# Cluster similarities of q and k in full float32, in four strips of 32 array columns

## The chip, the cores and the metric

The kernel runs on one core of a Trainium2 chip. Its engines are TensorE (PE in the rows, PEld for its weight loads), VectorE (DVE), ScalarE (ACT), GpSimd (POOL) and SyncE (SP), which here only issues DMAs. The metric is the device time of one execution in microseconds (us), as the median of several runs. The profile is of one execution of its own.

## What is computed

Clustered attention (2 batches, 8 heads, 768 positions, head size 64), followed by two gated feed-forward stages. The change touches the first lines of the attention only.

```python
q_n = q / (np.linalg.norm(q, axis=-1, keepdims=True) + 1e-06)
k_n = ...                                    # as q_n
c_n = ...                                    # the 16 centroids of each head
q_assign = np.argmax(np.einsum('bhsd,hcd->bhsc', q_n, c_n), axis=-1)
k_assign = np.argmax(np.einsum('bhsd,hcd->bhsc', k_n, c_n), axis=-1)
mask = q_assign[:, :, :, None] == k_assign[:, :, None, :]
scores = np.where(mask, scale * np.matmul(q, k.transpose(0, 1, 3, 2)), -1e9)
attn = softmax(scores)
x = attn @ v
...                                          # (x @ w1) * (x @ w2) @ w3 @ w_out, then the gated stage
```

A position belongs to the cluster whose centroid has the largest similarity. Positive factors of q and k don't change an argmax, so the kernel normalizes the centroids alone.

## The kernel before

**Pairs and blocks.** The 16 heads of both batches are handled as 8 pairs of heads (`pr` 0 to 7, the two heads `e` 0 and 1 on partitions 0 to 63 and 64 to 127). A block is 256 queries of one head; a pair has six, `at` 0 to 5, and the loop of L561 runs over 48 blocks `i` and a few more that fill and empty the pipeline. Each pass of the loop writes the instructions of all engines in a fixed order by hand, and each engine runs its own in that order.

**One block.** TensorE makes the scores of 128 queries at a time: `scores(2i+3)` at the start of the pass, `scores(2i+4)` in its second half, four matmuls each into one PSUM tile `s` (L323 to L326). DVE takes the row maximum `nm` (L333), ACT the exponential `e` (L344). TensorE transposes `e` (L354, tiles `pt`, three groups of four), ACT and DVE or GpSimd split the transposed weights into a high part `ph` (rounded to the short format fp32r) and a low part `pl` (L372, L383, L54, L59), and TensorE multiplies both by the values (L395, L396, tile `av`). ACT copies `av` out (L404). Products of fp32r parts stand in for float32 products all through the kernel.

**PSUM buffers.** The scores and the similarities take turns in one pool, `ps_s`, of two buffers. A tile waits until the last reader of the tile before last is done: normally the exponential of the scores two tiles earlier.

**Preparing a pair.** q and k of a pair are loaded as `raw` (L175; L172 for pair 1), and split into high and low parts `hi`, `lo` (`prep_split`, L191; for pair 1 into unused room of `x_hl`, `prep_split_1`, L206). SP moves the parts into the operand tiles `QH`, `KH`, `QX`, `KX` of each head (`prep_scatter`, L217). The similarities (`prep_sims`, L240) are eight matmuls from the parts and the centroid weights `cw`. `cw` has, for q and for k, 32 columns a head: 16 of the centroids' high part and 16 of their low part. The result `sims` has 128 rows (q and k, two heads, two parts) of 768 positions. DVE transposes it in squares of 32 (L255), the two parts are added (L261, on DVE for pair 0, else on GpSimd), and an argmax with its one-hot code follows (L268 to L282). The one-hot `oh` is padded to 32 columns a head and position group and transposed back (L286, `ohT`). `prep_mask` (L289) brings 32 rows of it under q's rows in `QH` and 32 under k's rows in `KH`, as 0 and a large negative number, so that the scores of other clusters fall far below. Pair 0, head 0 does this on ACT and DVE, everything else by DMA after one GpSimd operation (L300).

**When.** For pair `later`, two ahead of the running one, the load is issued at `at` 0, the split is made at `at` 3 and 4, the similarities at the end of `at` 5. For the next pair, DVE's transpose follows at `at` 0, the argmax at 1, the one-hot at 2, the masks at 3. Pair 0 is prepared before the loop, pair 1 in its first passes: its similarities stand in pass -1.

**Weights of the later stages.** They arrive as 64-bit words and are converted in the background of the attention (`f64_steps`, L88 to L120). For the first matrix DVE uses the unused end of a score tile in PSUM as scratch (L106 to L108), in the passes `at` 4 and 5 of pair 0.

Of the kernel before, what the change touches and what calls it, by code (L numbers as in the profile page):

```python
# [27 lines left out]
def tile_cluster_attention__then__moe__then__gated_moe(  # L28
# [123 lines left out]
    chi, clo = early[:, 256:384].bitcast(F32R), early[:, 384:512].bitcast(F32R)  # L152
    for j in range(2):
        nc.sync.dma_start(c2[:, j, :], centroids.rearrange("h c d -> (h c) d"))
    cw = cent.tile([128, NP, 2, 128], F32R, name="cw")
    nc.gpsimd.memset(cw.bitcast(F32), 0.0)
    dec = cent.tile([128, C], F32, name="dec")
    nc.gpsimd.iota(dec, [[-1, C]], base=C, channel_multiplier=0, allow_small_or_imprecise_dtypes=True)
    oh = cent.tile([128, S // 32, 32], F32, name="oh")
    nc.gpsimd.memset(oh, 0.0)  # L160
# [45 lines left out]
    def prep_split_1(engine):  # L206
# [6 lines left out]
        nc.gpsimd.tensor_scalar(out=q, in0=raw.pop((1, 0)), scalar1=0.125, scalar2=1.0, op0=ALU.mult, op1=ALU.mult)  # L213
        for w, x in ((0, q), (1, raw.pop((1, 1)))):
# [62 lines left out]
    def prep_onehot(pr):  # L277
# [950 lines left out]
```

## Time and profile before

| | us |
|---|---|
| median of 3 runs (758.78 to 759.42) | 759.25 |
| span of the profiled execution | 757.2 |
| TensorE busy in it | 745.6 |
| DVE busy | 575.9 |
| ACT busy | 469.4 |
| GpSimd busy | 424.3 |

The span runs from the first to the last instruction; the runs' times hold some 2.1 us more around it. The attention fills about the first 240 us, the feed-forward stages the rest. TensorE's busy time counts matmuls that overlap in the pipeline, so a busy TensorE says that it always had work, and a row's duration is longer than the step from one matmul's start to the next one's. The chain that ended last names, back from the last instruction, what each step waited for. In the rows below, a bracket at a line's end is the idle time of the engine just before, and what ended it.

### The profile page before, as it was taken

What the parts mean: (1) busy time and instruction counts of PE and PEld (TensorE: products, weight loads), DVE (VectorE), ACT (ScalarE), POOL (GpSimd) and SP (SyncE); (2) the same over time, 40 slices, a digit from 0 to 9 for tenths busy, and PEclk for the clock granted to TensorE, in tenths of its full rate; (3) what the DMA queues carried; (4) which work ended last, traced back from release to release, by engine and by line L of the source; (5) the groups of instructions that cost most, each with busy time, mean ns of one, the idle gap of its engine ahead of it and who ended that gap; (6) DMA issues with size and microseconds to landing.
All of it is one profiled execution on the core that took longest, in us unless ns stands there. A gap on an engine that the chain in (4) does not pass through costs nothing.

```text
span 757.2 us, 12243 instructions
## 1 busy us (share of the span) xinstructions
PE 745.6 (98%) x4283; PEld 680.0 (90%) x4283; DVE 575.9 (76%) x891; ACT 469.4 (62%) x990; POOL 424.3 (56%) x427
## 2 busy tenths in 40 slices
PE   7989999999999999999999999999999999999998
PEld 6879999999998888888888999999999999999996
DVE  6889989999987776766763386676687978869675
ACT  4779889888986545545442355676756555565630
POOL 3759888888873656433231036675547646375510
PEclk9999999999999999999999999999999999999999
DMA  7776867776623434333330001221302113030004
GB/s 194 204 197 173 200 169 189 192 185 161 175 60 119 140 114 158 124 134 139 113 123 17 1 1 56 84 84 56 112 0 98 70 57 112 14 121 34 29 0 168
DMA packets 29277, 82.83 MB, mean 109 GB/s; under 512 B 4864, under 2 KB 5536, under 8 KB 29216
## 3 DMA queue, kind: packets, MB, share of 16 engines
q1 hardware_dynamic: 29216, 82.05, 36.9%
q8 instruction: 34, 0.56, 0.3%
q14 instruction: 27, 0.22, 0.1%
HBM read 52.49 MB, written 3.19 MB: 74 GB/s over the span
## 4 chain that ended last, share of the span: by engine, by line
PE 93%; ACT 2%; DVE 2%; DMA 1%; issue 1%; SPq 1%; ACTq 0%; DVEq 0%
PE p L66 13%; PE p L67 13%; PE p L65 13%; PE pt L354 7%; PE p_a L66 4%; PE p_a L67 4%; PE p_a L65 4%; PE av L396 4%; PE av L395 4%; PE s L323 3%; PE s L325 3%; PE p_b L65 2%; PE p_b L66 2%; PE p_b L67 2%; PE w34p L66 2%; PE w34p L65 2%
## 5 line engine op out<-in xcount | busy, mean ns | idle before, releaser
L344 ACT ACTIVATE e<-s,nm 128x768 f32<-128x768 f32 x96 | 88.0, 917 | 16.9 <-DVE nm L333 14.0
L333 DVE TENSOR_REDUCE nm<-s 128x1 f32<-128x768 f32 x96 | 90.7, 945 | 7.8 <-PE s L326 7.1
L354 PE MATMUL pt<-ident,e 128*128 128x128 f32 x576 | 86.0, 272 | 0.0
L383 DVE TENSOR_TENSOR pl<-pt,ph 128x512 fp32r<-128x512 f32 x113 | 75.8, 682 | 10.9 <-ACT ph L372 10.1
L395 PE MATMUL av<-ph,vx 128*128 128x256 f32 x288 | 81.1, 308 | 0.3 <-POOL pl L59 0.3
L67 PE MATMUL p<-x,w 128*128 128x512 f32 (+1 forms) x208 | 80.1, 385 | 0.0
L66 PE MATMUL p<-x,w 128*128 128x512 f32 (+1 forms) x208 | 80.0, 385 | 0.0
L65 PE MATMUL p<-x,w 128*128 128x512 f32 (+1 forms) x208 | 80.0, 385 | 0.0
L116 POOL TENSOR_TENSOR w_a<-w_f 128x512 uint32<-128x512 uint32 x30 | 32.1, 1070 | 77.7 <-DVE w_f L115 39.3
L396 PE MATMUL av<-pl,vx 128*128 128x256 f32 x288 | 74.4, 287 | 0.6 <-DVE pl L383 0.5
L354 PEld LDWEIGHTS pt<-ident,e 128*128 128x128 f32 x576 | 67.8, 140 | 4.1
L372 ACT CAST ph<-pt 128x512 fp32r<-128x512 f32 x113 | 64.4, 588 | 7.1 <-PE pt L354 7.0
L1107 DVE TENSOR_TENSOR acc<-p,acc 128x512 f32<-128x512 f32 x59 | 40.5, 687 | 29.3 <-PE p L67 29.0
L923 POOL TENSOR_TENSOR wgv_a<-wgv_f 128x512 uint32<-128x512 uint32 x24 | 25.3, 1053 | 66.6 <-DVE wgv_f L922 38.4
L1001 ACT COPY s<-p_a 128x384 f32<-128x384 f32 x72 | 34.5, 478 | 43.1 <-PE p_a L67 42.8
L67 PE MATMUL p<-wo,u 128*128 128x512 f32 (+1 forms) x146 | 57.3, 393 | 0.0
L66 PE MATMUL p<-wo,u 128*128 128x512 f32 (+1 forms) x146 | 57.1, 391 | 0.0
L396 PEld LDWEIGHTS av<-pl,vx 128*128 128x128 f32 x288 | 54.7, 190 | 2.1 <-DVE pl L383 1.6
L65 PE MATMUL p<-wo,u 128*128 128x512 f32 (+1 forms) x146 | 56.3, 386 | 0.0
L395 PEld LDWEIGHTS av<-ph,vx 128*128 128x128 f32 x288 | 54.4, 189 | 1.4 <-POOL pl L59 0.5
L59 POOL TENSOR_TENSOR pl<-pc,ph 128x512 fp32r<-128x512 f32 x31 | 47.8, 1542 | 2.6
L323 PE MATMUL s<-KH,QH 96*128 96x512 f32 x96 | 42.8, 446 | 4.4 <-ACT e L344 2.1
(253 smaller groups left out, 2304.4 us busy)
## 6 DMA issues: line engine op xcount, KB each, us to landing
wgv_f<-in_w_gv_dram SPq DMA_DIRECT2D x24, 512.0 KB, 3.1
wo_f<-in_w_out_dram SPq DMA_DIRECT2D x20, 512.0 KB, 3.2
w_f<-in_w_dram SPq DMA_DIRECT2D x16, 512.0 KB, 3.1
w_f<-in_w3T_dram SPq DMA_DIRECT2D x16, 512.0 KB
raw<-in_qkT_dram SPq DMA_DIRECT2D x16, 384.0 KB, 4.9
r<-r_dram SPq DMA_DIRECT2D x16, 192.0 KB, 3.6
xb<-xa SPq DMA_DIRECT2D x15, 192.0 KB, 2.7
out_dram<-acc SPq DMA_DIRECT2D x11, 256.0 KB, 2.3
```

The costliest lines, as they stand in the source:

```text
L59: lo_engine.tensor_tensor(out=lo, in0=x, in1=hi, op=ALU.subtract)
L65: nc.tensor.matmul(ps, whi, xhi, start=start, stop=False, skip_group_check=more)
L66: nc.tensor.matmul(ps, whi, xlo, start=False, stop=False, skip_group_check=more)
L67: nc.tensor.matmul(ps, wlo, xhi, start=False, stop=stop, skip_group_check=more)
L323: nc.tensor.matmul(sp[:, 0:512], QH[:, q], KH[:, 0:512], start=True, stop=False)
L333: nc.vector.tensor_reduce(out=nms[j], in_=sps[j][:, 0:S], axis=AX.X, op=ALU.max, negate=True)
L344: nc.scalar.activation(et, sps.pop(j)[:, 0:S], AF.Exp, bias=nms.pop(j), accum_out=acc_x[pr, "sum"][:, at : at + 1])
L354: nc.tensor.transpose(pt[:, kk, 128 * t : 128 * t + 128], exps[2 * i + t][:, k0 : k0 + 128], ident)
L372: nc.scalar.copy(ph, pt)
L383: nc.vector.tensor_tensor(out=pl, in0=src, in1=ph, op=ALU.subtract)
L395: nc.tensor.matmul(avs[i], w, ph[:, kk, :], start=kt == 0, stop=False)
L396: nc.tensor.matmul(avs[i], w, pl[:, kk, :], start=False, stop=kt == KT - 1)
```

## The change

The similarities are computed by float32 matmuls from `raw` as loaded, with `cw` in float32. One matmul takes q or k of half of the positions, 384 columns, against 32 weight columns (16 centroids of each head), and writes one quarter of the partitions: strip 0 and 1 are q's halves, 2 and 3 are k's. The result is 128 rows of 384 columns. DVE's transpose of it gives the sums directly, so the split of the centroids, the eight copies into `cw` (now two) and the addition are gone. The one-hot has 16 columns a head, its transpose 384 columns, and the masks 16 rows: each mask is moved in two halves of the positions, so there are four moves a head. The first matmuls of the scores use 80 rows in place of 96. Pair 1's `raw` comes from the pool of the others, three buffers. In pairs 2 to 7 the similarities are written at the end of `at` 4 and DVE's transpose at `at` 5, one block earlier than before. The warm-up has 20 transposes fewer.

```diff
-    cw = cent.tile([128, NP, 2, 128], F32R, name="cw")
-    nc.gpsimd.memset(cw.bitcast(F32), 0.0)
+    cw = cent.tile([128, NP, 2 * C], F32, name="cw")
+    nc.gpsimd.memset(cw, 0.0)
...
-    oh = cent.tile([128, S // 32, 32], F32, name="oh")
-    nc.gpsimd.memset(oh, 0.0)
+    oh = cent.tile([128, S // 32, C], F32, name="oh")
...
     def load_qk(pr):
         for w in range(2):
-            if pr == 1:
-                raw[pr, w] = core.tile([128, S], F32, tag="e", name=f"raw{pr}_{w}", bufs=5)
-                nc.sync.dma_start(raw[pr, w], qkT[pr, :, w, :])
-                continue
             t = core.tile([128, S], F32, tag="raw", name=f"raw{pr}_{w}", bufs=3)
...
+    HALF = S // 2
     def prep_sims(pr):
-        hp = pr % NP
-        qh, ql, kh, kl = opnd[pr, "hl"]
         sp = ps_s.tile([128, 1024], F32, tag="s", name=f"sims{pr}")
-        ops = [(0, qh), (1, kh), (0, ql), (1, kl)]
-        for i, (w, t) in enumerate(ops):
-            for c0, c1 in ((0, 512), (512, 768)):
-                nc.tensor.matmul(sp[:, c0:c1], cw[:, hp, w, :], t[:, c0:c1], start=i == 0, stop=i == 3)
+        for n in range(4):
+            w, half = divmod(n, 2)
+            rows, cols = slice(32 * n, 32 * n + 32), slice(HALF * half, HALF * half + HALF)
+            nc.tensor.matmul(sp[rows, 0:HALF], cw[:, pr % NP, :], raw[pr, w][:, cols], start=True, stop=True)
+        del raw[pr, 0], raw[pr, 1]
...
     def prep_sum(pr):
         sp = opnd.pop((pr, "sims"))
-        sT = core.tile([128, S // 32, 32], F32, tag="raw", name=f"sT{pr}", bufs=3)
-        nc.vector.transpose(out=sT.rearrange("p j c -> p (j c)"), in_=sp[:, 0:S])
-        opnd[pr, "sT"] = sT
-
-    def prep_add(pr):
-        sT = opnd.pop((pr, "sT"))
         sm = core.tile([128, S // 32, C], F32, tag="sm", name=f"sm{pr}", bufs=1)
-        lead(pr).tensor_tensor(out=sm, in0=sT[:, :, 0:C], in1=sT[:, :, C : 2 * C], op=ALU.add)
+        nc.vector.transpose(out=sm.rearrange("p j c -> p (j c)"), in_=sp[:, 0:HALF])
...
     def prep_turn(pr):
-        ohT = core.tile([128, S], F32, tag="raw", name=f"ohT{pr}", bufs=3)
+        ohT = core.tile([128, HALF], F32, tag="ohT", name=f"ohT{pr}", bufs=1)
...
-        if pr == 0:
-            nc.gpsimd.tensor_scalar(out=ohT[96:128], in0=ohT[96:128], scalar1=-1.0, scalar2=BIG, op0=ALU.add, op1=ALU.mult)
-        if e == 0:
+        if e == 0 or pr == 0:
             nc.gpsimd.tensor_scalar(out=ohT[64:128], in0=ohT[64:128], scalar1=-1.0, scalar2=BIG, op0=ALU.add, op1=ALU.mult)
-        move(QH[64:96], ohT[32 * e : 32 * e + 32])
-        move(KH[64:96], ohT[64 + 32 * e : 96 + 32 * e])
+        for h in range(2):
+            at = 32 * h + C * e
+            move(QH[64 : 64 + C, halves[h]], ohT[at : at + C])
+            move(KH[64 : 64 + C, halves[h]], ohT[64 + at : 64 + at + C])
...
-            first = nxt and at == 0
-            if first:
+            summed = later if at == 5 else nxt if i == 0 else None
+            if summed:
                 split_lo(i - 1, 2)
-                prep_sum(nxt)
+                prep_sum(summed)
...
-            if later and at == 5:
+            if later and at == 4:
                 prep_sims(later)
```

On TensorE, in the second pair, the similarities of pair 3 (`sims3`) stand before the change behind the last transposes of the pair's sixth block (`pt11_2`), ahead of the scores `s27`:

```order
L354 MATMUL pt11_2_1195<-ident_60,e23_1085 128x128
L249 MATMUL sims3_1209<-hi3_0_1020,cw_114 128x512
L249 MATMUL sims3_1209<-hi3_0_1020,cw_114 128x256
L249 MATMUL sims3_1209<-hi3_1_1089,cw_114 128x512
L249 MATMUL sims3_1209<-hi3_1_1089,cw_114 128x256
L249 MATMUL sims3_1209<-lo3_0_1021,cw_114 128x512
L249 MATMUL sims3_1209<-lo3_0_1021,cw_114 128x256
L249 MATMUL sims3_1209<-lo3_1_1090,cw_114 128x512
L249 MATMUL sims3_1209<-lo3_1_1090,cw_114 128x256
L323 MATMUL s27_1218<-KH2_0_714,QH2_0_713 128x512
```

After it they stand behind the fifth block's last transposes (`pt10_2`), ahead of `s25`:

```order
L344 MATMUL pt10_2_1083<-ident_60,e21_982 128x128
L242 MATMUL sims3_1097<-raw3_0_746,cw_114 32x384 x2
L242 MATMUL sims3_1097<-raw3_1_748,cw_114 32x384 x2
L313 MATMUL s25_1102<-KH2_0_687,QH2_0_686 128x512
L314 MATMUL s25_1102<-KH2_0_687,QH2_0_686 128x256
```

Eight matmuls have become four, they read the loaded tiles in place of the split ones, and the scores behind them, which share the two PSUM buffers with them, are others.

On DVE, from the centroids to pair 0's masks, before the change (`lo0` are the low parts of q and k, `sT0` the transposed similarities, `sm0` their sums and then the code, `ohT0` the transposed one-hot):

```order
L58 CAST early_111<-cps_134 128x128
L59 TENSOR_TENSOR early_111<-cps_134,early_111 128x128
L510 CAST cw_114<-early_111 64x4x16 x4
L519 SCALAR_TENSOR_TENSOR lo0_0_146<-raw0_0_120,hi0_0_145 128x768
L520 TENSOR_TENSOR lo0_1_148<-raw0_1_122,hi0_1_147 128x768
L255 STREAM_TRANSPOSE sT0_257<-sims0_164 128x768
L261 TENSOR_TENSOR sm0_259<-sT0_257 128x384
L268 TENSOR_REDUCE mx0_261<-sm0_259 128x24
```

and after it:

```order
L495 COPY cw_114<-cps_133 64x4x16 x2
L497 SCALAR_TENSOR_TENSOR lo0_0_141<-raw0_0_119,hi0_0_140 128x768
L498 TENSOR_TENSOR lo0_1_143<-raw0_1_121,hi0_1_142 128x768
L249 STREAM_TRANSPOSE sm0_224<-sims0_151 128x384
L256 TENSOR_REDUCE mx0_226<-sm0_224 128x24
```

The cast, the subtraction, two of the four copies and the addition are gone, and the transpose is half as wide; what follows up to the mask keeps its order.

On SP, the mask moves of pair 3 between the load of its values and the load of the sums, before:

```order
L182 DMA vraw3_1395<-in_v_dram 128x768
L62 DMA QH3_0_1167<-ohT3_1433 32x768
L62 DMA KH3_0_1168<-ohT3_1433 32x768
L62 DMA QH3_1_1309<-ohT3_1433 32x768
L62 DMA KH3_1_1310<-ohT3_1433 32x768
L443 DMA r1_1464<-r_dram_65 64x768 x2
```

and after:

```order
L176 DMA vraw3_1353<-in_v_dram 128x768
L62 DMA QH3_0_1138<-ohT3_1391 16x384
L62 DMA KH3_0_1139<-ohT3_1391 16x384
L62 DMA QH3_0_1138<-ohT3_1391 16x384
L62 DMA KH3_0_1139<-ohT3_1391 16x384
L62 DMA QH3_1_1267<-ohT3_1391 16x384
L62 DMA KH3_1_1268<-ohT3_1391 16x384
L62 DMA QH3_1_1267<-ohT3_1391 16x384
L62 DMA KH3_1_1268<-ohT3_1391 16x384
L433 DMA r1_1426<-r_dram_65 64x768 x2
```

Four moves have become eight of a quarter of the size, and the two loads behind them stand four issues later.

## Rows read from the trace of the kernel before

**Rows 1.** The page: busy us, share and instructions by engine; the chain by engine.

```profile
PE 745.6 (98%) x4283; PEld 680.0 (90%) x4283; DVE 575.9 (76%) x891; ACT 469.4 (62%) x990; POOL 424.3 (56%) x427
...
PE 93%; ACT 2%; DVE 2%; DMA 1%; issue 1%; SPq 1%; ACTq 0%; DVEq 0%
```

**Rows 2.** Windows: length; busy us of PE, PEld, DVE, ACT, POOL; clock, DMA, GB/s.

```profile
24.00:52.00 28.00, 25.14 (x179) 22.54 (x178) 25.87 (x38) 23.17 (x50) 17.10 (x18) 1.00 0.80 199
...
75.00:102.00 27.00, 27.00 (x204) 25.29 (x203) 25.02 (x36) 23.58 (x52) 22.86 (x21) 1.00 0.75 184
```

**Rows 3.** Timeline (start, duration, engine, line): similarities of pairs 3 and 7.

```profile
77.11 0.93 PE L249 MATMUL sims<-hi,cw 128*128 128x512 f32 x4
...
77.64 0.90 ACT L344 ACTIVATE e<-s,nm 128x768 f32<-128x768 f32 x1 [0.24 <-DVE rt L435]
...
78.69 0.50 PE L323 MATMUL s<-KH,QH 96*128 96x512 f32 x1
...
184.87 0.94 PE L249 MATMUL sims<-hi,cw 128*128 128x512 f32 x4
```

**Rows 4.** Timeline of PE: four matmuls of scores, up to the next transposes.

```profile
70.70 0.40 PE L323 MATMUL s<-KH,QH 96*128 96x512 f32 x1
...
71.41 0.60 PE L354 MATMUL pt<-ident,e 128*128 128x128 f32 x4
```

**Rows 5.** Timeline of PE: the warm-up's float32 transposes.

```profile
9.02 6.28 PE L137 MATMUL warm<-ident 128*128 128x128 f32 x56
```

**Rows 6.** Timeline of ACT, DVE and PE through a pair's fourth and fifth block.

```profile
65.49 1.06 ACT L372 CAST ph<-pt 128x512 fp32r<-128x512 f32 x2
66.92 0.91 ACT L344 ACTIVATE e<-s,nm 128x768 f32<-128x768 f32 x1 [0.37 <-DVE nm L333]
...
71.41 1.35 DVE L200 SCALAR_TENSOR_TENSOR lo<-raw,hi 128x768 fp32r<-128x768 f32 x1
...
72.30 0.82 ACT L56 CAST hi<-raw 128x768 fp32r<-128x768 f32 x1
...
72.33 0.60 PE L354 MATMUL pt<-ident,e 128*128 128x128 f32 x4
...
72.68 0.48 PE L323 MATMUL s<-KH,QH 96*128 96x512 f32 x1
...
73.76 0.91 ACT L344 ACTIVATE e<-s,nm 128x768 f32<-128x768 f32 x1
```

**Rows 7.** Timeline of DVE: the one-hot's transpose and the maximum behind it.

```profile
64.48 0.97 DVE L286 STREAM_TRANSPOSE ohT<-oh 128x768 f32<-128x768 f32 x1
...
65.95 0.94 DVE L333 TENSOR_REDUCE nm<-s 128x1 f32<-128x768 f32 x1
```

**Rows 8.** The start: timeline of DVE, chain by time (start, us), one window.

```profile
9.22 0.98 DVE L255 STREAM_TRANSPOSE sT<-sims 128x768 f32<-128x768 f32 x1 [0.71 <-PE sims L249]
...
11.00 6.04 DMA raw<-in_qkT_dram
...
17.07 0.84 ACT x L210
...
9.00:10.00 1.00, 1.00 (x11) 1.00 (x10) 0.78 (x1) 0.00 (x0) 0.00 (x0) 1.00 1.00 215
```

**Rows 9.** Timeline of DVE and PE in pair 0 (brackets: idle before).

```profile
34.76 0.97 DVE L286 STREAM_TRANSPOSE ohT<-oh 128x768 f32<-128x768 f32 x1
...
43.20 0.48 PE L323 MATMUL s<-KH,QH 96*128 96x512 f32 x1
...
46.74 0.47 PE L323 MATMUL s<-KH,QH 96*128 96x512 f32 x1 [0.70 <-DVE w_f L108]
...
51.79 0.47 PE L323 MATMUL s<-KH,QH 96*128 96x512 f32 x1 [1.21 <-DVE w_f L108]
```

**Rows 10.** Timeline of SP: a mask's issue; DMA view: its median us to landing.

```profile
67.75 0.53 SPq L62 DMA_DIRECT2D KH<-ohT  x1
...
KH<-ohT SPq DMA_DIRECT2D x15, 96.0 KB, 2.1
```

More of the change, by code (lines that the diff above doesn't have):

```diff
@@ L212, in prep_split_1 @@
         q = core.tile([128, S], F32, tag="e", name="q1", bufs=5)
-        nc.gpsimd.tensor_scalar(out=q, in0=raw.pop((1, 0)), scalar1=0.125, scalar2=1.0, op0=ALU.mult, op1=ALU.mult)
-        for w, x in ((0, q), (1, raw.pop((1, 1)))):
+        nc.gpsimd.tensor_scalar(out=q, in0=raw[1, 0], scalar1=0.125, scalar2=1.0, op0=ALU.mult, op1=ALU.mult)
+        for w, x in ((0, q), (1, raw[1, 1])):
             nc.gpsimd.tensor_tensor(out=spare(3, w), in0=x, in1=spare(2, w), op=ALU.subtract)
@@ L291, in prep_mask @@
         QH, KH, _, _ = opnd[pr, e]
+        halves = [slice(HALF * h, HALF * h + HALF) for h in range(2)]
         if pr == 0 and e == 0:
-            nc.vector.tensor_scalar(out=KH[64:96], in0=ohT[64:96], scalar1=-1.0, scalar2=BIG, op0=ALU.add, op1=ALU.mult)
-            for cols in (slice(0, 256), slice(256, S)):
-                nc.scalar.copy(QH[64:96, cols], ohT[0:32, cols])
+            for h in range(2):
+                nc.vector.tensor_scalar(out=KH[64:96, halves[h]], in0=ohT[64 + 32 * h : 96 + 32 * h], scalar1=-1.0, scalar2=BIG, op0=ALU.add, op1=ALU.mult)
+                nc.scalar.copy(QH[64:96, halves[h]], ohT[32 * h : 32 * h + 32])
             return
-        if pr == 0:
-            nc.gpsimd.tensor_scalar(out=ohT[96:128], in0=ohT[96:128], scalar1=-1.0, scalar2=BIG, op0=ALU.add, op1=ALU.mult)
-        if e == 0:
+        if e == 0 or pr == 0:
             nc.gpsimd.tensor_scalar(out=ohT[64:128], in0=ohT[64:128], scalar1=-1.0, scalar2=BIG, op0=ALU.add, op1=ALU.mult)
-        move(QH[64:96], ohT[32 * e : 32 * e + 32])
-        move(KH[64:96], ohT[64 + 32 * e : 96 + 32 * e])
+        for h in range(2):
+            at = 32 * h + C * e
+            move(QH[64 : 64 + C, halves[h]], ohT[at : at + C])
+            move(KH[64 : 64 + C, halves[h]], ohT[64 + at : 64 + at + C])
     def prep_v(pr, e):
@@ L322, in scores @@
         sp = ps_s.tile([128, 1024], F32, tag="s", name=f"s{j}")
-        nc.tensor.matmul(sp[:, 0:512], QH[:, q], KH[:, 0:512], start=True, stop=False)
-        nc.tensor.matmul(sp[:, 512:S], QH[:, q], KH[:, 512:S], start=True, stop=False)
+        rows = slice(0, D + C)
+        nc.tensor.matmul(sp[:, 0:512], QH[rows, q], KH[rows, 0:512], start=True, stop=False)
+        nc.tensor.matmul(sp[:, 512:S], QH[rows, q], KH[rows, 512:S], start=True, stop=False)
         nc.tensor.matmul(sp[:, 0:512], QX[:, q], KX[:, 0:512], start=False, stop=True)
@@ L497, in tile_cluster_attention__then__moe__then__gated_moe @@
     nc.tensor.transpose(cps, c2.rearrange("p j d -> p (j d)"), ident)
-    warm(8, "warm1")
-    def spread_cent(g, src, engine):
-        for e in range(2):
-            rows = slice(64 * e, 64 * e + 64)
-            for w in range(2):
-                base = 64 * w + 32 * e
-                out = cw[rows, :, w, base + 16 * g : base + 16 * g + 16]
-                x = src[rows].bitcast(F32).rearrange("p (n e c) -> p n e c", n=NP, e=2)[:, :, e, :]
-                if engine is nc.scalar:
-                    nc.scalar.copy(out, x)
-                else:
-                    engine.tensor_copy(out, x)
+    warm(4, "warm1")
     hl = [core.tile([128, S], F32R, tag=tag, name=f"{tag}0_{w}", bufs=2) for w in range(2) for tag in ("hi", "lo")]
@@ L514, in tile_cluster_attention__then__moe__then__gated_moe @@
     nc.scalar.activation(hl[0], raw[0, 0], AF.Copy, scale=0.125)
-    split(cps, chi, clo, nc.vector, nc.vector)
-    spread_cent(0, chi, nc.scalar)
-    spread_cent(1, clo, nc.vector)
+    for e in range(2):
+        rows = slice(64 * e, 64 * e + 64)
+        x = cps[rows].rearrange("p (n e c) -> p n e c", n=NP, e=2)[:, :, e, :]
+        nc.vector.tensor_copy(cw[rows, :, C * e : C * e + C], x)
     nc.scalar.copy(hl[2], raw[0, 1])
     nc.vector.scalar_tensor_tensor(out=hl[1], in0=raw[0, 0], scalar=0.125, in1=hl[0].bitcast(F32), op0=ALU.mult, op1=ALU.subtract)
-    nc.vector.tensor_tensor(out=hl[3], in0=raw.pop((0, 1)), in1=hl[2], op=ALU.subtract)
-    raw.pop((0, 0))
+    nc.vector.tensor_tensor(out=hl[3], in0=raw[0, 1], in1=hl[2], op=ALU.subtract)
     nc.scalar.activation(nrm[:, 0:1], nrm[:, 3:4], AF.Exp)
     prep_sims(0)
-    warm(56, "warm2")
+    warm(40, "warm2")
     prep_scatter(0, 0)
@@ L628, in tile_cluster_attention__then__moe__then__gated_moe @@
                 turn_sums(pr, sps[2 * i + 4][:, S : S + 128])
-            if nxt and at == 0:
-                prep_add(nxt)
             if nxt and at == 1:
```

6 lines of the change are left out of this document (2 added, 4 removed).

## The prediction

> **What bounds the kernel now.** I read the busy times and the chain that ended last first: TensorE is busy 745.6 us of a span of 757.2 and makes up 93% of the chain [rows 1]. Then the windows, because the change touches the attention alone. From 75 to 102 us, one head pair long, TensorE is busy all 27.00 us, DVE 25.02 and ACT 23.58; from 24 to 52 us TensorE is busy 25.14 of 28 and DVE 25.87 [rows 2]. So the attention has two regimes: up to about 52 us DVE and ACT set the pace, and from there to the end TensorE does. In the second a microsecond counts only where it is TensorE's.
>
> A pair lasts 26.94 us there: five pairs' similarities start between 77.11 and 184.87, four steps apart [rows 3]. At the place of the similarities TensorE goes from 77.11 to the next scores at 78.69: **1.58 us** [rows 3]. Most of that is the eight matmuls, and at its end is a wait: the next scores take the PSUM buffer that the exponential of 77.64 + 0.90 = 78.54 still reads, and start 0.15 after it [rows 3]. Whatever the new similarities cost, they have to be set against these 1.58 us, and against whatever exponential stands behind them at their new place.
>
> **The similarities themselves, in TensorE's time.** Removed: eight fp32r matmuls, 3072 columns a pair. Added: four float32 matmuls of 384 columns, 1536 columns, each in its own 32 array columns. No row shows such a matmul, nor matmuls that share the array, so I bound it by two rows. 1536 columns of fp32r scores take 71.41 - 70.70 = 0.71 us [rows 4]. Plain float32 data went through once in the warm-up, 56 transposes in 6.28 us, 112 ns for 128 columns [rows 5], or 1.34 us for 1536 columns. The kernel before needs four fp32r products (high and low part of both operands) for what is now one float32 product, so an estimate of the upper price is four passes, 4 x 0.71 = 2.84 us, with the strips one after another; with four strips at once it is 0.71. Between these: if a strip is two half-price steps in order and the next strip can start beside the second one, 5/8 of 2.84 = 1.78; if it is four quarter steps, 13/16 of it = 2.31. I take something up to 1.78, and keep 0.7 and 2.84 for the range.
>
> The Trainium skill (TensorE: Matmul & The Clock Gate, Part 3: Packing small matmuls) says that matmuls in different column groups run beside each other, started and ended strictly in order, 2.38 times as fast for three tiles of 32 columns; FP8 and Floating Point Precision (TensorE Precision Notes) gives true float32 four passes. By both the price would be at most 2.84 / 2.38 = 1.2 us, an estimate; no run here shows either yet. The Trainium skill's TensorEngine Tiling (Array Packing), Key Properties, speaks against the change: a switch of tiling mode drains the array, which would happen twice a pair. It gives no price and no row here shows one; up to 0.4 us in all it would leave the sum below as it is.
>
> **Where they stand now.** They move from the end of a pair's sixth block to the end of its fifth, 72.33 + 0.35 = 72.68 in this pair, where today the next scores start at once [rows 6]. Two PSUM buffers are shared by scores and similarities, so the scores behind the similarities must now wait for the exponential of the scores just ahead of them. In the fifth block that exponential is late: ACT has the 0.82 us cast of the later pair's k ahead of it, DVE the 1.35 us low part of its q, and it runs from 73.76 to 74.67 [rows 6]. At today's times the next scores would start at 74.67 + 0.15 = 74.82, 2.14 us behind 72.68, however short the similarities are.
>
> Something of this comes back. ACT runs without a gap from the exponential at 66.92 to that at 73.76; that one had waited 0.37 us for a row maximum [rows 6], which started at 65.95 on DVE behind the 0.97 us transpose of the one-hot [rows 7]. That transpose is now half as wide, some 0.42 us less by its two widths. The casts ahead of the 66.92 exponential end at 65.49 + 1.06 = 66.55 [rows 6], so the chain moves up by 0.35, and the scores start at 74.82 - 0.35 = 74.47: **1.79 us** behind 72.68. The similarities are hidden as long as they take less than 1.79 - 0.15 = 1.64 us. Against 1.58 that is +0.21 us a pair, for five pairs (the similarities from 77 us on, pairs 3 to 7): **+1.05 us**. The floor of this wait, with DVE and ACT free at once: scores end near 71.6, 0.94 for the maximum, 0.91 for the exponential, three hand-overs, 73.6: 0.95 us. The ceiling is 2.14.
>
> **The first 52 us.** The start of the scores moves forward: no split of the centroids, two copies in place of eight, no addition, two transposes of half width. The DVE chain that begins with the transpose at 9.22 [rows 8] begins earlier and is some 1.4 us shorter inside. It buys little, because ACT's first exponentials stand behind the scaling of the second pair's q and k, whose load lands at 11.00 + 6.04 = 17.04 and is used at 17.07 [rows 8]. The DMA engines are full from 7 us on (share 1.00 at 9 to 10 us [rows 8]), so an earlier issue brings the landing forward by little. I take nothing here, bounds 0 and -0.7. From 25 to 44 us DVE has no gaps, and the one-hot's transpose at 34.76 [rows 9] stands on the chain: -0.35, bounds 0 and -0.5. The GpSimd addition that goes (one a pair) ended no wait of TensorE's.
>
> Near 46 and 51 us TensorE waits 0.70 and 1.21 us for the weight conversion, which uses the end of a score buffer as scratch [rows 9]. With the similarities one block earlier, the buffer order shifts: the scores that start at 43.20 today [rows 9] will wait for the conversion, near 46.7, and the second wait falls on scores two places later, which come late enough. From 46.7 the work of a block and a half (scores 0.75, transposes 0.44, products 1.05, scores 0.7, the rest 1.5) leads to the scores now at 51.79 by 51.2: -0.55, bounds +0.3 and -0.8. These similarities lie under the wait, at any price up to 3.4 us. Sum of the start: **-0.9 us**, from +0.3 to -2.0.
>
> **The masks.** Two moves a head become four of a quarter of the size; four more issues a pair on SP, of about 0.55 us. The last mask piece of a pair's first head is issued 1.1 us later. In the pair around 68 us the piece is issued at 67.75, lands some 2.1 us after that, and its scores start at 70.70 [rows 4, 10]; the GpSimd work ahead of it is on half the columns, so this is a tie: +0.1. In the later pairs GpSimd is not behind and the issue is earlier, which covers it. Behind these issues queue only the loads of the sums and of the later pair, which are early. Fewer contraction rows (80 for 96), a smaller zero fill and 20 warm-up transposes fewer cost and give nothing: columns set a matmul's time, and the rest lies under the load.
>
> **Sum.** -0.9 + 0.1 + 1.05 = +0.25 us on a span of 757.15, 757.4. The median of the runs is 2.1 us above the span (759.25), which the change doesn't touch: **759.5 us**.
>
> **Rivals.** First, the strips don't run together (the change doesn't do what it says): 2.84 us a pair, scores 0.15 later at 2.99, +1.41 for five pairs = +7.05, and +0.4 at the second pair's similarities near 20 us; with -0.8 from the rest +6.65, **765.9 us**. It decides from 1.64 us on. For it: nothing in the trace shows two matmuls at once. In between, two half steps give 1.93, +0.35 for five pairs, 760.2, which I count with the forecast; four quarter steps give 2.46, +0.88 for five, 762.9.
>
> Second, the wait at the new place shrinks, because DVE has less to do in the third and fifth block and the exponentials come sooner than ACT's row suggests. At the floor, 0.95 + 0.15 of similarities or wait, about 1.0 us: -0.58 for five pairs = -2.9, with -0.8 **755.5 us**; half way, 757.5. Against it: ACT is without a gap for 7.7 us before that exponential, and the change takes nothing off ACT there.
>
> By the skill's rule of strips side by side the first rival falls and 759.5 or the second stands; by its rule of four passes without overlap it is 765.9.
>
> **How the numbers follow.** The forecast with two half steps 0.50; quarter steps 0.10; strips one after another 0.17; the shorter wait 0.18; masks or start off by more than bounded 0.05. A measurement of this kernel tells about 0.2%, 1.5 us. Faster by more than that (below 757.7) 0.17, from the shorter wait; within it 0.50; slower (above 760.8) 0.33, from the slow strips and the upper part of the forecast's own spread. The range leaves out the lower part of the second rival and half of the first: 756.5 to 765.5.
>
> **What would show it.** Right: scores start 1.7 to 2.0 us after the fifth block's last transposes, their idle time ended by ACT's exponential; pairs of about 27.1 us; no wait at the sixth block; first exponentials still near 17.8. Wrong: float32 matmuls that start one after another, with the scores released by TensorE itself; pairs of 26.4 us or less; a first exponential before 17 us; scores at a pair's start that wait for a mask's DMA.

## The result and the profile after

| | before | after |
|---|---|---|
| median, us | 759.01 (4 runs, 758.71 to 759.42) | 768.15 (4 runs, 765.08 to 768.53) |
| span of the profiled execution | 757.2 | 763.2 |
| time of that execution | 759.25 | 765.08 |

The changed kernel is slower: ratio 1.0113, 95% interval 1.0095 to 1.0131. The forecast was 759.5 us with a range up to 765.5, so it was wrong by 8.65 us, and the time lies outside its range. The profiled execution of after is the shortest of the four; the other three have spans of 765.9 to 766.6 at a mean granted clock of 0.989 in place of 0.993.

The page of after, TensorE's line and the chain by engine (answering [rows 1]):

```profile
PE 743.5 (97%) x4263; PEld 672.5 (88%) x4263; DVE 576.8 (76%) x887; ACT 468.4 (61%) x986; POOL 411.7 (54%) x419
...
PE 84%; ACT 5%; DVE 3%; DMA 3%; issue 2%; SPq 2%; POOL 1%; DVEq 0%; ACTq 0%; POOLq 0%
```

TensorE is 84% of the chain where it was 93%: more of the time is now waiting for other engines. Where, the starts of the scores tell, numbered from 0 (their lines are L323 before, L313 after; profiled executions; us):

| scores | before | after | after - before | since the row above |
|---|---|---|---|---|
| 0 | 15.60 | 12.84 | -2.76 | shorter centroid chain |
| 2 | 18.85 | 18.07 | -0.78 | waits for the first exponential |
| 5 | 25.07 | 26.80 | +1.73 | TensorE at half its clock |
| 10 | 36.82 | 38.08 | +1.26 | half-width one-hot transpose |
| 15 | 51.79 | 52.24 | +0.45 | other place of the conversion wait |
| 24 | 70.70 | 72.45 | +1.75 | second pair: the clash told below, and 0.36 for a mask |
| 27 | 78.69 | 80.48 | +1.79 | pair 3's similarities |
| 36 | 97.64 | 99.99 | +2.35 | |
| 39 | 105.62 | 108.38 | +2.76 | pair 4's similarities |
| 75 | 186.42 | 192.13 | +5.71 | three more pairs, 0.98 each |
| 87 | 211.62 | 217.86 | +6.24 | last one-hot; from here on no change |

So of the 6.0 us of span 0.45 are there at 52 us, and the pairs add the rest. In a later pair (scores 27 to 39, 39 to 51 and so on) these are 0.56 us between the similarities and 0.41 us at them.

Windows of after at the start (columns as in [rows 2]; before has a clock of 1.00 in all of these):

```profile
14.00:16.00 2.00, 0.52 (x4) 0.20 (x2) 1.67 (x2) 0.84 (x1) 0.77 (x1) 1.00 0.83 305
16.00:18.00 2.00, 0.00 (x0) 0.00 (x0) 0.00 (x0) 1.70 (x4) 1.92 (x3) 0.58 1.10 230
18.00:20.00 2.00, 1.93 (x8) 1.25 (x12) 0.24 (x1) 0.90 (x3) 2.00 (x2) 0.50 1.02 240
...
26.00:28.00 2.00, 2.00 (x16) 1.91 (x14) 1.56 (x3) 1.43 (x4) 1.08 (x1) 0.86 1.07 295
```

Timelines of PE and ACT of after (start, duration, engine, line; the bracket is the idle time before and what ended it), answering [rows 3, 6, 8, 9]:

```profile
12.84 0.47 PE L313 MATMUL s<-KH,QH 80*128 80x512 f32 x1 [1.37 <-ACT QH L284]
...
16.30 0.84 ACT L204 ACTIVATE x<-raw 128x768 fp32r<-128x768 f32 x1 [0.35 <-DMA raw<-in_qkT_dram]
17.05 0.88 ACT L334 ACTIVATE e<-s,nm 128x768 f32<-128x768 f32 x1
...
18.07 0.80 PE L313 MATMUL s<-KH,QH 80*128 80x512 f32 x1 [3.56 <-ACT e L334]
...
48.00 0.47 PE L313 MATMUL s<-KH,QH 80*128 80x512 f32 x1 [2.51 <-DVE w_f L108]
...
72.45 0.47 PE L313 MATMUL s<-KH,QH 80*128 80x512 f32 x1 [0.21 <-DMA KH<-ohT]
...
74.66 0.85 PE L242 MATMUL sims<-raw,cw 128*32 128x384 f32 x8
76.22 0.50 PE L313 MATMUL s<-KH,QH 80*128 80x512 f32 x1 [0.70 <-ACT e L334]
...
130.04 0.85 PE L242 MATMUL sims<-raw,cw 128*32 128x384 f32 x8
132.02 0.50 PE L313 MATMUL s<-KH,QH 80*128 80x512 f32 x1 [1.13 <-ACT e L334]
```

The first scores came 2.76 us earlier and then waited 3.56 us for an exponential that stands on ACT behind the scaling of pair 1's q and k and their load. In that gap the granted clock went to half (1.2 GHz) and stayed there until 26.5 us: the first scores matmul takes 0.80 us at 18.07 and 0.47 at 12.84. At the similarities the wait is the forecast one, for the exponential: their step to the next scores is 1.56 us at 74.66 and 1.98 at 130.04.

Nothing in the prediction stands for the 0.56 us a pair. Timelines of DVE, POOL, ACT and PE of after at the argmax of the third pair:

```profile
87.56 1.28 POOL L59 TENSOR_TENSOR pl<-pc,ph 128x512 fp32r<-128x512 f32 x1
87.68 1.57 DVE L257 TENSOR_TENSOR sm<-sm,mx 128x384 f32<-128x384 f32 x1
89.17 0.94 DVE L323 TENSOR_REDUCE nm<-s 128x1 f32<-128x768 f32 x1
...
90.15 0.90 ACT L334 ACTIVATE e<-s,nm 128x768 f32<-128x768 f32 x1 [1.14 <-DVE nm L323]
...
90.48 0.28 PE L385 MATMUL av<-ph,vx 128*128 128x256 f32 x1
90.77 0.38 PE L386 MATMUL av<-pl,vx 128*128 128x256 f32 x1
```

And the same place before, with the one pair of before in which GpSimd came first:

```profile
28.13 1.29 POOL L59 TENSOR_TENSOR pl<-pc,ph 128x512 fp32r<-128x512 f32 x1
28.17 1.67 DVE L269 TENSOR_TENSOR sm<-sm,mx 128x384 f32<-128x384 f32 x1
...
85.92 0.56 DVE L269 TENSOR_TENSOR sm<-sm,mx 128x384 f32<-128x384 f32 x1
86.00 1.63 POOL L59 TENSOR_TENSOR pl<-pc,ph 128x512 fp32r<-128x512 f32 x1
```

DVE's comparison of the argmax and GpSimd's subtraction `pl` start within 0.12 us of each other. Whichever starts second is held. DVE first: comparison 0.56 us, subtraction 1.60 to 1.63. GpSimd first: subtraction 1.28, comparison 1.57 to 1.67. The comparison comes once while each of the first seven pairs runs. Before, DVE is first by 0.07 to 0.10 us in the last six; after, GpSimd is first by 0.04 to 0.12 us in all seven. The lost microsecond reaches the next row maximum, its exponential (1.14 us of idle ACT) and a product that waits for `pl` (it starts at 90.77; 0.12 us behind the one ahead of it, like its neighbours, would be 90.60).

The Trainium skill (SBUF — State Buffer, Who interferes with whom) says it as a rule: a DVE operation with two inputs in SBUF and a GpSimd operation that reads SBUF take turns by a lock, and the order of issue decides who waits. These rows agree, with 1.0 us on DVE's side and 0.35 on GpSimd's.

### The profile page after: what moved, and what is told of

Read it like the earlier page. It is cut to its first block, busy times and chain, and to the rows that moved or that the text cites. A ratio compares the mean times of both kernels' runs of the same rounds, so it can differ in the third digit from the quotient of the medians.

```text
span 763.2 us, 12267 instructions
## 1 busy us (share of the span) xinstructions
PE 743.5 (97%) x4263; PEld 672.5 (88%) x4263; DVE 576.8 (76%) x887; ACT 468.4 (61%) x986; POOL 411.7 (54%) x419
## 4 chain that ended last, share of the span: by engine, by line
PE 84%; ACT 5%; DVE 3%; DMA 3%; issue 2%; SPq 2%; POOL 1%; DVEq 0%; ACTq 0%; POOLq 0%
PE p L67 13%; PE p L66 13%; PE p L65 13%; PE pt L344 5%; PE p_a L66 4%; PE p_a L65 4%; PE p_a L67 4%; PE av L386 3%; PE av L385 3%; ACT e L334 2%; PE s L313 2%; PE p_b L65 2%; PE p_b L66 2%; PE p_b L67 2%; PE w34p L66 2%; PE w34p L65 2%
## 5 line engine op out<-in xcount | busy, mean ns | idle before, releaser
L323 DVE TENSOR_REDUCE nm<-s 128x1 f32<-128x768 f32 x96 | 91.0, 948 | 15.8 <-PE s L316 14.6
L313 PE MATMUL s<-KH,QH 80*128 80x512 f32 x96 | 43.9, 458 | 13.4 <-ACT e L334 7.8
L59 POOL TENSOR_TENSOR pl<-pc,ph 128x512 fp32r<-128x512 f32 x31 | 45.7, 1475 | 2.6
```

Of the source, the lines that this page charges most:

```text
L59: lo_engine.tensor_tensor(out=lo, in0=x, in1=hi, op=ALU.subtract)
L313: nc.tensor.matmul(sp[:, 0:512], QH[rows, q], KH[rows, 0:512], start=True, stop=False)
L323: nc.vector.tensor_reduce(out=nms[j], in_=sps[j][:, 0:S], axis=AX.X, op=ALU.max, negate=True)
```

## The experiments

Theory A: the lower clock costs the start. Theory B: without GpSimd's addition, GpSimd comes first in that clash. Theory C: the new place of the similarities costs the pairs. In the diffs `warm` writes warm-up transposes, work without a use. Edits named a_ are made to the changed kernel, those named b_ to the kernel before; ratios are to the kernel before, run beside each.

**a_fill: keep TensorE busy.**

```diff
-    warm(40, "warm2")
+    warm(52, "warm2")
...
+            if i == -1:
+                warm(32, "warm3")
             scores(2 * i + 4)
```

> The changed kernel with 52 warm-up transposes behind the first similarities in place of 40, and 32 more behind the second scores, so that TensorE has work while it waits for the first exponentials. Theory A (the clock): the changed kernel loses its start because TensorE stands idle from 14.4 to 18.1 us and its granted clock falls to half until 26.5 us; here the clock stays at 1.00, the sixth scores start near 24.3 us in place of 26.8, and the time falls from 768.2 to 762 to 763. If the clock had nothing to do with it, the time stays at 768.

764.58 us (762.99 to 765.76), ratio to before 1.0077 [1.0062, 1.0092]: 3.6 less than after, and short of the forecast. Scores 5 start 1.27 us ahead of before where after was 1.73 behind, so A holds for the start: 3.0 us. Only 1.3 of it were left at scores 15, because the clock now fell at the next gap, that of the weight conversion: from scores 13 to 15 it takes 5.81 us, where a_best below, at 1.00, takes 4.24. A line of its timeline of PE, and two of its windows (columns as above):

```profile
45.09 0.61 PE L313 MATMUL s<-KH,QH 80*128 80x512 f32 x1 [2.24 <-DVE w_f L108]
```

```profile
44.00:46.00 2.00, 0.91 (x3) 0.84 (x4) 1.90 (x4) 0.44 (x1) 0.86 (x1) 0.82 0.26 68
46.00:48.00 2.00, 2.00 (x10) 1.90 (x10) 0.99 (x2) 0.55 (x2) 0.00 (x0) 0.50 0.87 194
```

This run also holds a test of the clash. In its third pair, and only there, DVE came first:

```profile
86.36 0.68 DVE L257 TENSOR_TENSOR sm<-sm,mx 128x384 f32<-128x384 f32 x1
...
86.72 1.47 POOL L59 TENSOR_TENSOR pl<-pc,ph 128x512 fp32r<-128x512 f32 x1
```

From scores 27 to 39 it lost 0.08 us against before, in each of the next three pairs 0.98 to 1.00.

**b_warm40: the shorter warm-up alone.** In the kernel before, 4 and 40 transposes in place of 8 and 56.

> The kernel before with the shorter warm-up of the changed one (4 and 40 transposes in place of 8 and 56) and nothing else. Its scores still start near 15.6 us, so TensorE stands idle some 2 us ahead of them. If the cut of the warm-up is by itself what lets the clock fall, the granted clock is 0.5 for some microseconds after 16 us and the time rises by 2 to 6 us, to 761 to 765. If it takes the gap of 3.6 us that the earlier scores opened, the clock stays at 1.00 and the time at 758.7.

760.48 us (759.38 to 761.82, 10 runs), 1.0018 [1.0009, 1.0028]. In eight of ten runs the clock fell (mean 0.995 or 0.996), in two it did not (1.000, 759.4 and 759.5). Windows of the profiled one:

```profile
18.00:20.00 2.00, 0.72 (x2) 0.63 (x3) 1.06 (x2) 1.90 (x5) 2.00 (x2) 0.54 1.01 229
20.00:22.00 2.00, 2.00 (x8) 1.71 (x7) 0.96 (x1) 0.10 (x2) 1.93 (x2) 0.50 1.04 248
```

So the cut alone already lets the clock fall, mostly. The profiled run is 1.87 us behind before at scores 5, and that is not made up; 0.66 of it is there at scores 0, ahead of the fall. The larger gap of the changed kernel isn't needed for the fall.

**a_fill_pool: GpSimd's work back.**

```diff
+            if nxt and at == 0:
+                sm = opnd[nxt, "sm"]
+                nc.gpsimd.tensor_tensor(out=sm, in0=sm, in1=sm, op=ALU.add)
```

> a_fill with a GpSimd addition (the similarities added to themselves, which changes no argmax) at the place where the kernel before had its addition. Theory B (the GpSimd order): without that addition GpSimd begins its subtraction pl just ahead of DVE's comparison of the argmax, and DVE's comparison takes 1.6 us in place of 0.56, which delays a row maximum, an exponential and two of TensorE's products by 0.57 us in each of six pairs. Expected: the comparison back at 0.56 us, and 3 us less than a_fill. Rival (only the moved similarities cost): the same time as a_fill.

759.10 us (758.48 to 760.72, 10 runs), 1.0008 [0.9999, 1.0017]: 5.5 us less than a_fill in the median and 3.7 in the profiled runs, more than the 3 that B asked. POOL and DVE in the fourth pair:

```profile
113.00 0.56 DVE L257 TENSOR_TENSOR sm<-sm,mx 128x384 f32<-128x384 f32 x1
...
113.08 1.63 POOL L59 TENSOR_TENSOR pl<-pc,ph 128x512 fp32r<-128x512 f32 x1
```

DVE is first again, by 0.08, and the comparison is back at 0.56 us in five of the seven pairs (0.90 in the third; in the first GpSimd is first, as it was before). From scores 27 to 75 the kernel loses 0.22 us against before, a_fill 3.05: an operation added to GpSimd saves 0.7 us a pair on TensorE. Part of what had looked like the cost of the place (theory C) went with it. At scores 87 the profiled runs differ by 3.98 us; the rest of the 5.5 lies in runs without a profile.

**b_noadd: the addition alone taken out of the kernel before.** The argmax reads the half of the centroids' high part only; the low part is left out.

```diff
-        lead(pr).tensor_tensor(out=sm, in0=sT[:, :, 0:C], in1=sT[:, :, C : 2 * C], op=ALU.add)
-        opnd[pr, "sm"] = sm
+        opnd[pr, "sm"] = sT[:, :, 0:C]
```

> The kernel before without the addition of the two halves (the argmax reads the high parts' half alone, so the low parts of the centroids are left out of the choice of cluster). Theory B: GpSimd comes to its subtraction 1 us earlier and ahead of DVE's comparison, which takes 1.6 us in place of 0.56 in each pair; the time goes up by 2 to 3 us, to 761 to 762. Rival (the addition ended no wait of TensorE, as predicted): 759.0 or up to 0.6 less for the DVE addition that goes in pair 0.

759.43 us (759.14 to 760.47, 10 runs), 1.0012 [1.0003, 1.0022], 0.75 us more than before. B in this form falls. DVE and POOL in the second and the third pair:

```profile
58.42 1.58 DVE L267 TENSOR_TENSOR sT<-sT,mx 128x384 f32<-128x384 f32 x1
...
86.37 0.56 DVE L267 TENSOR_TENSOR sT<-sT,mx 128x384 f32<-128x384 f32 x1
...
58.31 1.27 POOL L59 TENSOR_TENSOR pl<-pc,ph 128x512 fp32r<-128x512 f32 x1
...
86.44 1.63 POOL L59 TENSOR_TENSOR pl<-pc,ph 128x512 fp32r<-128x512 f32 x1
```

Of the six pairs in which DVE was first before, only the one at 58 us turned, and only there 1.0 us were lost (scores 19 to 22); elsewhere DVE stayed first by 0.06 to 0.07. Taking the addition off isn't enough, since GpSimd then waits for ACT's copy `pc` (its `ph` starts at 85.73 after 0.92 us idle). In the changed kernel that copy also comes earlier, 0.2 us by the scores' offset of 2.72. ACT before, then after, in the fourth pair:

```profile
111.51 0.62 ACT L369 COPY pc<-pt 128x512 f32<-128x512 f32 x1
```

```profile
114.04 0.62 ACT L359 COPY pc<-pt 128x512 f32<-128x512 f32 x1
```

0.06 us of margin less 0.2 gives an order turned by some 0.1, as measured. That both together turn it is read from these rows; no run moves the copy alone, and why it comes earlier is open.

**b_delay: theory B', the order itself.** In the kernel before, one DVE operation of 0.15 us ahead of the comparison.

```diff
+        if pr > 0:
+            nc.vector.tensor_scalar(out=mx[:, 0:1], in0=mx[:, 0:1], scalar1=1.0, scalar2=None, op0=ALU.mult)
         nc.vector.tensor_tensor(out=sm, in0=sm, in1=mx.unsqueeze(2).broadcast_to(shape), op=ALU.is_ge)
```

> The kernel before with one tiny DVE operation (128 x 1, some 0.15 us) put ahead of the argmax's comparison in pairs 1 to 7, and nothing else. Theory B': DVE's comparison and GpSimd's subtraction start within 0.1 us of each other, and the one that starts second is held. In the kernel before DVE is first by 0.07 to 0.10 us; 0.15 us later it is second, takes 1.6 us in place of 0.56, and each of five to six pairs loses 0.6 us: 3 us or more, 762. Rival: the operation costs DVE its own 0.15 us and nothing on TensorE's path: 758.8.

766.12 us (766.09 to 766.28), 1.0099 [1.0082, 1.0115]: 7.4 us from seven operations of 0.15 us, at a clock of 1.000. Timelines of POOL, DVE, ACT and PE:

```profile
86.97 0.15 DVE L270 TENSOR_SCALAR mx<-mx 128x1 f32<-128x1 f32 x1
87.06 1.29 POOL L59 TENSOR_TENSOR pl<-pc,ph 128x512 fp32r<-128x512 f32 x1
87.16 1.60 DVE L271 TENSOR_TENSOR sm<-sm,mx 128x384 f32<-128x384 f32 x1
...
89.66 0.90 ACT L346 ACTIVATE e<-s,nm 128x768 f32<-128x768 f32 x1 [1.39 <-DVE nm L335]
...
90.28 0.39 PE L398 MATMUL av<-pl,vx 128*128 128x256 f32 x1 [0.24 <-DVE pl L385]
```

The comparison is second by 0.10 us and takes 1.60; scores fall back 1.2 us in each of the six pairs whose order turned (+1.04 at scores 27, +2.27 at 39, +7.20 at 87). B' holds; the size was forecast too small.

**a_late: the argmax behind the block's second row maximum.**

```diff
-            if nxt and at == 1:
-                prep_argmax(nxt)
...
             maxima(2 * i + 4)
+            if nxt and at == 1:
+                prep_argmax(nxt)
+                prep_code(nxt)
```

> a_fill with the argmax (maximum and comparison) moved behind the second row maximum of the same block, where GpSimd's subtraction is over, and no GpSimd addition. Theory B': the comparison takes 0.56 us, no product waits for pl, and the time is that of a_fill_pool, 759. If it was GpSimd's lateness as such, not the clash of the two, that helped in a_fill_pool, the time stays at a_fill's 764.6.

765.14 us (763.16 to 765.72), 1.0080 [1.0065, 1.0095]: no gain. The comparison is at 0.56 us, but GpSimd's work moved too, and the clash came back one operation on, at the one-hot (POOL and DVE):

```profile
91.74 1.28 POOL L59 TENSOR_TENSOR pl<-pc,ph 128x512 fp32r<-128x512 f32 x1
...
92.36 1.08 DVE L270 TENSOR_TENSOR oh<-sm,mc 128x384 f32<-128x384 f32 x1
```

The one-hot takes 1.08 us where it took 0.56 before. 0.56 us are lost there, between scores 33 and 34, and none between 30 and 33, where after loses 0.32 behind the comparison. The time is the rival's, though by the same clash at another pair of operations.

**a_fill_old: the old place.** Similarities at `at` 5, DVE's transpose at the next pair's `at` 0.

> a_fill with the similarities back at the end of a pair's sixth block and DVE's transpose back at the next pair's first block. Theory C (the place): at the sixth block TensorE's step past the similarities is again 1.6 us, as with eight matmuls before, in place of 2.0; 0.4 us less in each of four pairs, -1.7 us against a_fill; the conversion waits of pair 0 fall as before the change. Under the theory that strips save TensorE their whole difference (0.85 us of bursts against 1.6) it would be 0.7 us a pair less, -3.5 us.

762.78 us (760.91 to 763.81), 1.0047 [1.0030, 1.0063]: 1.8 less than a_fill, as C had it, but the parts don't bear C out alone. From scores 27 to 75 it loses 1.81 us against before, a_fill 3.05, so beside the clash the place is worth 0.3 us a pair; the clash stays (comparison 1.59 to 1.66 in six of seven pairs), so the place isn't what turned the order. Its start was another one in the profiled run, 1.9 us later: the warm-up ran slowly until 11 us (7 or 8 transposes per us, later 12, while the clock column reads 1.00 throughout), and the 52 transposes themselves held the first scores back to 14.72, where a_fill's start at 12.85. In the profiled runs of a_late, a_best2 and a_best3 they start at 14.34 to 14.64 likewise: the fill has a price in some executions.

**a_double: every matmul of the similarities twice, on a_fill_pool.**

> a_fill_pool with every matmul of the similarities done twice, so that a pair's strips take about 1.7 us in place of 0.85. If they lie under the wait for the exponential, as the prediction has it (hidden up to 1.64 us), the scores behind them start as in a_fill_pool, the idle time ahead of them shrinks from 0.8 to 1.1 us to 0.2 or less, and the time stays at 759.1. If they were on TensorE's path, 0.85 us in each of five pairs: 763.4.

760.08 us (758.52 to 762.66, 10 runs), 1.0021 [1.0009, 1.0033]. PE of a_fill_pool, then of a_double, pair 6's similarities:

```profile
153.64 0.85 PE L242 MATMUL sims<-raw,cw 128*32 128x384 f32 x8
155.33 0.50 PE L313 MATMUL s<-KH,QH 80*128 80x512 f32 x1 [0.83 <-ACT e L334]
```

```profile
155.72 0.85 PE L242 MATMUL sims<-raw,cw 128*32 128x384 f32 x8
156.38 0.83 PE L246 MATMUL sims<-raw,cw 128*32 128x384 f32 x8
157.40 0.50 PE L317 MATMUL s<-KH,QH 80*128 80x512 f32 x1 [0.19 <-ACT e L338]
```

The step to the scores is 1.69 and 1.68 us: twice the work, the same time. The second set starts 0.66 us behind the first, so a set of four strips costs TensorE 0.66 us. From scores 27 to 75 a_double loses 0.14 us against before, a_fill_pool 0.22. The 2.0 us between the two profiled runs are all there at scores 15 (+1.01 and -1.00; scores 2 at +0.79 and -0.69): the similarities of pairs 0 and 1 were doubled too, and the warm-up ran more slowly.

**a_best, a_best2, a_final, a_best3: can it win?** a_best is a_fill_pool with pairs 3 to 7's similarities at the old place, pair 2's at the new one, and 20 transposes under the conversion wait.

> a_fill_pool with the similarities of pairs 3 to 7 back at the end of the sixth block (pair 2's stay at the fifth, under the conversion wait) and 20 warm-up transposes behind pair 2's similarities, so that TensorE has work during that wait. Expected: no clock loss at 46 to 50 us, 0.3 to 0.4 us less in each of four pairs: 757.0 to 757.7, a microsecond below the kernel before. Rival: the order of DVE's comparison and GpSimd's subtraction turns again (comparison 1.6 us) and takes it back, 759 to 761.

760.27 us (758.43 to 761.33, 10 runs), 1.0016 [1.0006, 1.0025]. The granted clock was 1.000 in all ten runs, and the lead at scores 15 was 2.42 us. Then the rival came (DVE and POOL in the fourth pair):

```profile
112.35 1.66 DVE L257 TENSOR_TENSOR sm<-sm,mx 128x384 f32<-128x384 f32 x1
...
112.31 1.28 POOL L59 TENSOR_TENSOR pl<-pc,ph 128x512 fp32r<-128x512 f32 x1
```

The comparison was second by 0.04 us, and 0.67 us were lost a pair. GpSimd's addition, of one tile to itself, takes 0.83 us where the old one took 1.01. That was not all: 1.4 us of the lead went between scores 23 and 24, where TensorE waited 1.26 us; the profile names a short ACT operation (L414), and no run settles the cause.

a_best2 moves pair 1's split behind the first exponentials.

> a_best with the split of pair 1 behind the first two exponentials in place of ahead of them (the similarities no longer need it). If ACT's place behind the loads of pair 1 is what kept the first exponentials at 17 us, they start near 15 us, the third scores near 16, and the lead of some 2 us holds up to the conversion wait near 43 us. If that wait's end is set by DVE's own chain the lead holds through it too: 755 to 756.5; if it is set by the load of the words, the lead is lost there: as a_best.

760.27 us (757.92 to 763.06, 10 runs), 1.0019 [1.0003, 1.0036]. It doesn't decide what the moved split is worth: the warm-up ran slowly in the profiled run, the first scores came at 14.64, and the first exponential at 16.62. The lead was 2.98 us at scores 15 and 3.09 at 27, and the fourth to the seventh pair lost nearly all of it to the clash again (comparison second by 0.04 to 0.06 us, 1.64 to 1.66 long).

a_final is a_best with a_late's argmax in place of the GpSimd operation.

> a_best with the later argmax in place of the GpSimd addition. a_best was 2.4 us ahead of the kernel before at 52 us and lost 0.7 us a pair to the clash of comparison and subtraction. Without the clash the lead holds: 756 to 757. If the loss of a_best in the pairs came from the old place of the similarities itself, 0.3 to 0.6 us a pair, it stays near 760.

761.59 us (760.70 to 762.94), 1.0039 [1.0027, 1.0051]: as in a_late, the clash moved to the one-hot (1.07 to 1.08 us), 0.55 us a pair.

a_best3 adds a second GpSimd operation to a_best.

```diff
                 nc.gpsimd.tensor_tensor(out=sm, in0=sm, in1=sm, op=ALU.add)
+                nc.gpsimd.tensor_scalar(out=sm, in0=sm, scalar1=1.0, scalar2=1.0, op0=ALU.mult, op1=ALU.mult)
```

> a_best with a second GpSimd operation (a multiplication by 1, some 0.5 us) behind its addition. In a_best DVE's comparison started 0.04 to 0.06 us behind GpSimd's subtraction and took 1.65 us. Theory B': with GpSimd 0.5 us later, the comparison is first by 0.4 us and takes 0.56, no pair loses 0.7 us, and the lead of 2.4 us that a_best had at 52 us holds to the end: 756 to 757.5, below the kernel before. Rival: GpSimd's subtraction, half a microsecond later, now makes TensorE's products wait, or the clash moves to another pair of operations, as it did to the one-hot in a_late: 759 to 762.

757.67 us (755.88 to 760.00, 12 runs), 0.9985 [0.9975, 0.9995]: faster than the kernel before, by 1.1 us. DVE and POOL in its fifth pair:

```profile
138.69 0.87 DVE L257 TENSOR_TENSOR sm<-sm,mx 128x384 f32<-128x384 f32 x1
...
139.24 1.47 POOL L59 TENSOR_TENSOR pl<-pc,ph 128x512 fp32r<-128x512 f32 x1
```

The comparison is first by 0.55 us in this pair and nowhere second. It isn't free: it takes 0.87 us, not the 0.56 expected, now beside GpSimd's `ph` (138.53, 0.63 us). The kernel is ahead of before by 0.70 us at scores 28 and by 1.45 at 88, so the pairs no longer lose. The median is just above the forecast of 756 to 757.5: the lead of 2.44 us at scores 15 had shrunk to 0.24 at scores 24, 1.4 of it at the wait of a_best.

## Why the prediction was wrong, point by point

**What bounds the kernel: half right.** TensorE sets the pace in the pairs, and its waits were followed to ACT's exponential. What DVE and GpSimd do to each other was not looked at. The rows were there: one comparison of 1.67 us at 28.17, GpSimd's `pl` of 1.63 us beside 1.29, and margins of at most 0.1 us between their starts in every pair.

**The price of the strips: right, and too careful.** Taken as up to 1.78 us, bounds 0.7 and 2.84; measured 0.66 us a pair (a_double), the price of one fp32r pass over 1536 columns (0.71 [rows 4]). 0.66 is a little under the lower bound, and counts nothing as long as it lies under the wait. The rival of strips one after another is refuted. By the page that the prediction cites (the Trainium skill, TensorE: Matmul & The Clock Gate, Part 3: Packing small matmuls) it would have been at most 1.2 us, an estimate, and 0.66 agrees with that bound. The step from the last transposes to the strips is 0.53 us in the changed kernel (74.13 to 74.66), where full-array matmuls followed 0.35 behind. A drain at a switch of tiling mode (the Trainium skill, TensorEngine Tiling (Array Packing), Key Properties) may be these 0.18 us; no run separates it from what else a first strip may cost, and they too lie under the wait.

**The wait at the new place: right in mechanism, too large in the sum.** Forecast 1.79 us, counted from 0.35 behind the start of the last transposes, and +0.21 a pair. Without the clash the step is 1.69 us from the strips' start in the last two pairs of a_fill_pool (1.00 to 1.98 in the others), or 1.87 counted as the forecast did. Between the scores on both sides of it (47 to 51, 59 to 63, 71 to 75) a_fill_pool loses 0.13 or 0.14 us against before, and it gains as much elsewhere: these three pairs cost 0.03 us less than before, not 0.21 more. In the changed kernel 0.41 a pair are lost at that place, with steps of 1.97 to 1.99 in three pairs of five, because the clash also makes the exponential late: a_fill loses 0.24 there in its pair without the clash and 0.42 in the next ones.

**"The GpSimd addition that goes (one a pair) ended no wait of TensorE's", and so counted nothing: the step that failed.** It ended none, but the step left out what the change does to the order of DVE's comparison and GpSimd's `pl`, a margin of 0.1 us. b_delay shows what that order is worth in the kernel before: 7.4 us for 0.15 us on DVE, seven times. In the changed kernel GpSimd work at the addition's place brings the order back in the five pairs from the second on in which a_fill had GpSimd first, and takes 5.5 us off the median (a_fill against a_fill_pool). The addition alone is not the whole cause: taken out of the kernel before, it turns one pair (b_noadd, 0.75 us). By the rows the earlier copy `pc` does the rest, which no run shows by itself.

**"20 warm-up transposes fewer cost and give nothing": the other step that failed.** The prediction has no term for TensorE's clock. Alone the cut costs 1.65 us in the median (b_warm40). In the changed kernel, with the earlier scores' longer gap, half the clock turned a lead of 0.78 us at scores 2 into 1.73 behind at scores 5; a_fill turned that into 1.27 ahead. No run gives back the 20 transposes alone in the changed kernel: a_fill adds 44. That the three other runs of after are 3.4 us longer at a mean clock of 0.989 may be a second such stretch at the conversion wait, as a_fill shows it; those runs have no profile, so it is not shown.

**The first 52 us: right in kind, too careful where the clock held.** The forecast was -0.9 us, at most -2.0; a_best, at a clock of 1.00, has -2.42 at scores 15, a_fill_pool, with the clock lost once, -1.00. The first exponentials were to stay near 17.8 behind the load, with a lead of 0 to 0.7 us; the load was used at 16.30, where before it was 17.07, the exponential came at 17.05, and with TensorE kept busy scores 5 are 1.2 to 1.4 us ahead (a_best, a_fill, a_fill_pool). The one-hot's transpose was to bring 0.35 (0.42, scores 9 to 10). The scores at 43.20 were to wait for the conversion to 46.7 and the scores at 51.79 to come 0.55 sooner: in a_best, with the clock kept, scores 12 to 16 gain 0.72; in a_fill_pool, with the clock lost in that wait, they lose 0.82.

**The masks: right place, somewhat more.** Forecast +0.1; the scores at 72.45 wait 0.21 us for a mask, and lose 0.36.

**The rivals.** None of those named came. The shorter wait didn't either. The rival that was missing is that order; it would have had its price in the row at 28.17, 1.1 us of DVE in each pair.

**Where the sum is met, it is partly luck.** With both failed steps countered, a_fill_pool has 759.10 us, near the forecast 759.5. But from scores 15 to 24 it loses 1.37 us where 0.1 was forecast (for the masks), and from there to scores 87 it gains 0.26 where 1.05 were to be lost.

## What to carry to other kernels

Before an operation is taken away from DVE or GpSimd, look for pairs of operations of the two that start together and have two durations in the trace: the order of such a pair may hang on 0.1 us, and work that ends no wait may be what keeps it. Dummy work that fills a gap of TensorE is part of the schedule; count which gap each piece covers and what it holds back itself, and look at the clock in the windows behind every gap that the change opens or lengthens. Start earlier only what the next engine can take: 2.76 us of earlier scores turned into a longer wait and a lower clock.

## What the runs showed of the hardware

- Four float32 matmuls of 384 columns in four strips of 32 array columns cost TensorE 0.66 us together; each shows as two records of 0.49 to 0.51 us.
- In the changed kernel the step from full-array transposes to the strips is 0.53 us, where it is 0.35 to full-array matmuls.
- A DVE operation on two SBUF tiles that starts 0.04 to 0.12 us behind a GpSimd subtraction of 1.28 us takes 1.57 to 1.67 us in place of 0.56 (after); one that starts 0.62 us behind takes 1.08 (a_late). The other way round, 0.07 to 0.10 us apart, GpSimd's takes 1.60 to 1.63 (before).
- TensorE's granted clock was at half (1.2 GHz) for 10.2 us from 16.3 us on, within an idle stretch of 3.56 us (after), and for 3.4 us from 45.3 us on, just behind one of 2.24 us (a_fill). Two idle stretches of 2.51 us differ: the one ahead of 48.00 left it at 1.00 (after), the one ahead of 45.00 was followed by 3.4 us at 0.50, from 46.0 us on (a_fill_pool). In b_warm40 it fell in eight runs of ten: the same kernel doesn't always pay.
